# Exponentials issued one block product behind the minima of their scores, in a fused attention and feed-forward kernel

## The chip, the cores and the metric

The kernel runs on one core of one Trainium2 chip. The metric is the time of one execution on the device in microseconds (us), as the median of several runs. The core has five engines that work side by side, each through its own list of instructions: PE (TensorE, matrix products; its weight loads are shown as PEld), DVE (VectorE), ACT (ScalarE), POOL (GpSimd) and SP (SyncE, which here only starts transfers). They wait for each other by semaphores.

## The reference

Sliding-window attention over 8 batches, 8 heads, 576 positions and 64 columns per head is followed by a feed-forward part in which three products are joined by their maximum.

```python
scores = (1/sqrt(64)) * q @ k.T                        # [8, 8, 576, 576]
rel = pos[:, None] - pos[None, :]
scores = where((rel >= 0) & (rel < 128), scores - slope[h] * abs(rel), -1e9)
attn = exp(scores - max(scores)); attn = attn / (sum(attn) + 1e-9)
x = (attn @ v)  -> rows of [4608, 512]
h = maximum(maximum(x @ w1, x @ w2), x @ w3)           # [4608, 768]
out = h @ w_out                                        # [4608, 512]
```

## The kernel before

**Attention.** A batch has four pairs of heads, and each pair five blocks of query rows: four of 128 and one of 64. One such block is a *step*; a batch has 20. For one step the work goes through these functions:

- `products` (L283): PE makes the scores of two blocks at a time, in PSUM. Because the window is 128 wide, each row needs 128 keys, taken from its own block and the one before.
- `score`: DVE merges the two blocks of keys into 128 columns (L298 or L301, a predicated copy), then for each of the two heads adds the bias and takes the row's minimum of the negated scores in one instruction (L313), which writes the tile `s` and one column of `st`. ACT then takes the exponential of `s` into the tile `p`, with that minimum as its bias, and sums each row into `st` (L317). The tiles `s` are a ring of three, the tiles `p` a ring of four.
- `sums_of`: for two blocks (one, for the last of a pair) DVE adds 1e-9 to the sums (L326) and takes reciprocals (L329).
- `normalise`: ACT multiplies `p` by the reciprocals, head by head (L341). In the first two batches POOL does it for half of the blocks (L336).
- `turn`: PE transposes `p` (L350) into the one tile `pt`, ACT copies it out (L354, L360, L363), and POOL cuts the two triangles of the window out of it (L364, L368).
- `mix`: PE multiplies with `v` (L390) into `ps_x`, and ACT copies the finished pair of heads to `xk` (L399).

**Feed-forward.** Each of the matrices is cut in blocks of two by two, and a product is made in seven block products by a scheme of Strassen's kind, so that per batch there are 11 x 7 = 77 *units*. A unit is one block product on PE: six matmuls of 128x288 for w1, w2 and w3, nine for w_out (L541). Numbers are split in a high and a low part: ACT casts the high part (L416), and DVE or POOL subtracts to get the low part (L417). The sums and differences of blocks are DVE's (L420). The results go into three PSUM banks in turn. The first three units of a product are copied out of their bank by ACT (L550), to be added again by DVE later (L490, L504, L507); L499 and L505 take the maximum over w1, w2 and w3, and L488 and L501 are copies on ACT. Unit results for w_out go to memory by SP.

**Weights.** At the start the weights are converted from 64-bit words on ACT and DVE (L137 to L145), split (L151, L152), combined on PE (L162) and stored by SP in device memory as `keep`; the w_out part stays on the core. Each batch after the first loads them again from `keep`, in two pieces per matrix, into a ring of two (L239, issued from POOL's queue when a piece has become free).

**What sets the order.** The program makes a list of events, each with a time in steps, sorts it and issues the work in that order. Step `s` is the block's number plus a shift per batch. `products` come at `s` (for two blocks), `score` at `s + 0.04`, `sums_of` at `s + 0.9`, `normalise` at `s + 1.3`, `turn` four steps behind the products and `mix` some six. The units of the batch before are spread over the same time line, one every 0.285 to 0.32 of a step. A scheduler then orders each engine's instructions, by priorities that follow the order of issue and by when it expects their inputs. From the end of the second batch's attention on PE's order is kept as the program has it (`fix`); the other engines' order stays the scheduler's.

The lines touched are L304 to L320 in `score` and the list of events, L578 to L581; what reads their results is L326, L329, L341 and the transposes L350. The lines that stand beside them on ACT and DVE, and on which PE waits, are L550, L416, L420, L499 and L504.

## Time and profile before

| | us |
|---|---|
| median of 3 runs | 832.92 (832.41 to 834.43) |
| the profiled execution's own time | 837.5 |
| its span in the profile | 835.4 |
| mean granted clock of PE in it | 0.987 of full speed |

The profile is one execution. Its times are in us from the start of the span. A row of the timeline has start, length, engine, line of the kernel, operation, output and input tiles, shapes and the number of instructions (x1), and in brackets how long the engine stood idle before it and which instruction, by engine, tile and line, released it. A row of the waits has the engine with the line that waited, what it waited for, and then us in total, number of waits and the longest. Rows of a table by stretches have the stretch, its length, and busy time with the number of instructions for each engine. A busy PE need not run at its peak, since the ends of its matmuls are modelled.

One batch takes 92.4 us in the steady part. The stages in the span: weights are prepared up to about 205 us, beside the attention of the first batches; the first batch's units for w1 to w3 run to about 280; four like batches follow from 320 to 690; from 690 the last one runs out. A matmul of L541 has a mean of 299 ns, an exponential L317 of 401 ns, a copy L550 of 395 ns.

### The profile page before, as it was taken

What the parts mean: (1) busy time and instruction counts of PE and PEld (TensorE: products, weight loads), DVE (VectorE), ACT (ScalarE), POOL (GpSimd) and SP (SyncE); (2) the same over time, 40 slices, a digit from 0 to 9 for tenths busy, and PEclk for the clock granted to TensorE, in tenths of its full rate; (3) what the DMA queues carried; (4) which work ended last, traced back from release to release, by engine and by line L of the source; (5) the groups of instructions that cost most, each with busy time, mean ns of one, the idle gap of its engine ahead of it and who ended that gap; (6) DMA issues with size and microseconds to landing.
All of it is one profiled execution on the core that took longest, in us unless ns stands there. A gap on an engine that the chain in (4) does not pass through costs nothing.

```text
span 835.4 us, 18318 instructions
## 1 busy us (share of the span) xinstructions
PE 786.7 (94%) x6488; PEld 692.4 (83%) x6488; DVE 564.2 (68%) x1758; ACT 530.3 (63%) x1728; POOL 325.1 (39%) x564
## 2 busy tenths in 40 slices
PE   4987999999999999999999999999999999999988
PEld 2555888789888898889888988889888899899987
DVE  5768999985666846775667847694767747674452
ACT  6779887865667756676557756775657666552332
POOL 2333252532345515542345416541444425531332
PEclk9969999999999999999999999999999999999999
DMA  7664378475877548783687558873787458656751
GB/s 250 212 229 133 125 284 291 164 265 163 266 267 265 192 151 282 261 274 126 232 290 256 195 196 273 273 263 127 245 280 253 170 190 269 246 186 201 272 172 57
DMA packets 43402, 184.81 MB, mean 221 GB/s; under 512 B 4784, under 2 KB 13744, under 8 KB 34096
## 3 DMA queue, kind: packets, MB, share of 16 engines
q0 software_dynamic: 18144, 115.61, 41.7%
q1 hardware_dynamic: 25024, 67.97, 23.1%
q8 instruction: 51, 0.84, 0.4%
q14 instruction: 39, 0.32, 0.1%
q10 hardware_dynamic: 144, 0.07, 0.0%
HBM read 157.68 MB, written 25.95 MB: 220 GB/s over the span
## 4 chain that ended last, share of the span: by engine, by line
PE 63%; DVE 12%; ACT 8%; DMA 6%; issue 5%; POOL 5%; SPq 0%; ACTq 0%; DVEq 0%; POOLq 0%
PE ps_m L541 43%; PE ps_x L390 7%; PE ps_s L283 5%; DMA wt<-keep 4%; PE pt L350 4%; POOL hs L417 4%; PE pt L162 3%; ACT p L317 2%; DVE t L420 2%; DMA hs<-in_w_all 2%; DVE t L504 2%; DVE hq L505 1%; PE ps_m L283 1%; DVE hq L420 1%; ACT p L341 1%
## 5 line engine op out<-in xcount | busy, mean ns | idle before, releaser
L541 PE MATMUL ps_m<-xs,wt 128*128 128x288 f32 x3024 | 435.1, 299 | 16.7 <-ACT t L550 5.4
L541 PEld LDWEIGHTS ps_m<-xs,wt 128*128 128x128 f32 x3024 | 409.1, 189 | 27.7 <-ACT t L550 7.5
L550 ACT COPY t<-ps_m 128x288 f32<-128x288 f32 x264 | 103.0, 395 | 84.4 <-PE ps_m L541 83.5
L364 POOL TENSOR_SCALAR_AFFINE_SELECT pp<-pr 128x256 f32<-128x256 f32 (+1 forms) x128 | 54.9, 429 | 244.3 <-ACT pr L363 143.3
L541 PE MATMUL ps_m<-hs,ow 128*128 128x288 f32 x1008 | 141.6, 297 | 7.1 <-POOL hs L417 3.4
L541 PEld LDWEIGHTS ps_m<-hs,ow 128*128 128x128 f32 x1008 | 134.5, 188 | 10.7 <-POOL hs L417 4.5
L317 ACT ACTIVATE p<-s,st 128x128 f32<-128x128 f32 (+1 forms) x320 | 127.2, 401 | 17.7 <-DVE st L313 12.1
L239 POOL DMA_DIRECT2D wt<-keep x126 | 70.1, 556 | 133.9 <-PE ps_m L541 124.1
L417 POOL TENSOR_TENSOR hs<-hq,hs 128x288 fp32r<-128x288 f32 x88 | 78.1, 896 | 67.7 <-ACT hs L416 67.3
L341 ACT ACTIVATE p<-p,st 128x128 f32<-128x128 f32 x280 | 96.8, 396 | 11.8 <-DVE st L329 11.8
L504 DVE TENSOR_TENSOR t<-ps_m,t 128x288 f32<-128x288 f32 x144 | 64.6, 453 | 49.3 <-PE ps_m L541 34.8
L313 DVE CUSTOM_DVE_ANT_0 s<-ps_s,bias 128x128 f32<-128x128 f32 (+1 forms) x300 | 76.7, 281 | 18.6 <-PE ps_s L283 12.5
L301 DVE COPY_PREDICATED ps_s<-prev,ps_s 128x256 f32<-128x256 uint8 x120 | 50.8, 423 | 50.2 <-PE ps_s L283 48.7
L390 PE MATMUL ps_x<-pp,v 128*64 128x256 f32 (+3 forms) x768 | 82.4, 332 | 1.8 <-POOL pp L364 1.4
L283 PE MATMUL ps_s<-qk 64*64 64x192 f32 (+1 forms) x1080 | 71.4, 333 | 6.3 <-DMA qk<-in_qk 4.2
L390 PEld LDWEIGHTS ps_x<-pp,v 128*64 128x64 f32 (+1 forms) x768 | 46.5, 140 | 28.1 <-issue 12.5
L505 DVE TENSOR_TENSOR hq<-t,hq 128x288 f32<-128x288 f32 x144 | 67.7, 478 | 2.4
L363 ACT COPY pr<-pt 128x256 f32<-128x256 f32 x64 | 18.9, 321 | 74.6 <-PE pt L350 74.6
L417 POOL TENSOR_TENSOR hs<-t,hs 128x288 fp32r<-128x288 f32 x64 | 58.9, 924 | 15.2 <-ACT hs L416 14.9
L350 PE MATMUL pt<-ident,p 128*128 128x128 f32 (+1 forms) x320 | 56.6, 289 | 7.6 <-POOL p L336 3.9
L317 ACT ACTIVATION_READ_ACCUMULATOR p<-s,st 128x1 f32 (+1 forms) x320 | 61.7, 193 | 0.0
L283 PEld LDWEIGHTS ps_s<-qk 64*64 64x64 f32 x1080 | 41.4, 136 | 23.6 <-issue 10.9
(68 smaller groups left out, 837.8 us busy)
## 6 DMA issues: line engine op xcount, KB each, us to landing
wt<-keep POOLq DMA_DIRECT2D x63, 1024.0 KB, 7.7
wt<-keep POOLq DMA_DIRECT2D x63, 768.0 KB, 5.0
qk<-in_qk SPq DMA_DIRECT2D x31, 576.0 KB, 5.4
hs<-in_w_all SPq DMA_DIRECT2D x24, 512.0 KB, 3.9
v<-in_v SPq DMA_DIRECT2D x32, 320.0 KB, 4.2
keep<-wt SPq DMA_DIRECT2D x9, 1024.0 KB, 5.1
outT<-t SPq DMA_DIRECT2D x64, 144.0 KB, 1.8
keep<-wt SPq DMA_DIRECT2D x9, 768.0 KB, 3.6
```

Source lines behind the costliest of these rows:

```text
L239: nc.gpsimd.dma_start(wts[n, a], keep[n % 9][a])
L283: pe(nc.tensor.matmul(ps[j][d:d + D, o:o + k1 - k0], lhsT=qkt[t][j * D:(j + 1) * D, 0, q0:q0 + D], rhs=qkt[t][j * D:(j + 1) * D, 1, k0:k1] ...
L313: nc.vector.tensor_tensor_reduce(out=s[:n], in0=ps[j][:n, P:2 * P], in1=(bias if i else bias0)[:n, 2 * hp + j, :], scale=-0.125, scalar=3. ...
L317: nc.scalar.activation(p[:n, j], s[:n], AF.Exp, bias=st[:n, 0, a, j:j + 1], scale=-1.0, accum_out=st[:n, 1, a, j:j + 1])
L341: nc.scalar.activation(p[:n, j], p[:n, j], AF.Copy, scale=st[:n, 2, a, j:j + 1])
L350: pe(nc.tensor.transpose(out=pt[:, a, j, :n], in_=p[:n, j], identity=ident[:n, :n]))
L390: pe(nc.tensor.matmul(x[j * D:(j + 1) * D, c:c + e - a], lhsT=vv[:n, i, j * D:(j + 1) * D], rhs=w[:n, j].rearrange("p a b -> p (a b)")[:, ...
L417: e.tensor_tensor(out=lo, in0=src, in1=hi.bitcast(F32), op=ALU.subtract)
L504: nc.vector.tensor_tensor(out=s, in0=ps, in1=e, op=ALU.add)
L505: nc.vector.tensor_tensor(out=h, in0=s, in1=h, op=ALU.max)
L541: pe(nc.tensor.matmul(ps, lhsT=lt, rhs=rt, start=i == 0 and k in (0, 1, 4), stop=i == len(pairs) - 1, skip_group_check=True,))
L550: nc.scalar.copy(out=e, in_=ps)
```

## The change

`score` keeps the merging and the two minima, and puts the two tiles `s` aside. A new function `exps` takes the tile `p` and issues the two exponentials. It is an event of its own at `s + 0.3`, where before the exponentials came at `s + 0.04` with the minima. With units about 0.3 of a step apart this lets one unit be issued between a block's minima and its exponentials. `sums_of` moves from `s + 0.9` to `s + 1.1` and `normalise` from `s + 1.3` to `s + 1.5`. Operations, sizes and rings stay the same.

```diff
-        p = s_p.tile([P, 2, P], F32, name="p", bufs=4)
...
         a = len(two)
-        two.append(p)
+        two.append(None)
+        less[t, i] = []
         for j in range(2):
             s = s_p.tile([P, P], F32, name="s", bufs=3)
             nc.vector.tensor_tensor_reduce(
...
             )
+            less[t, i].append(s)
+
+    less = {}
+
+    def exps(t, i):
+        n = rows[i]
+        st, two = stats[t, i // 2]
+        a = i % 2
+        p = two[a] = pn[t, i] = s_p.tile([P, 2, P], F32, name="p", bufs=4)
+        for j, s in enumerate(less.pop((t, i))):
             nc.scalar.activation(
                 p[:n, j], s[:n], AF.Exp, bias=st[:n, 0, a, j:j + 1], scale=-1.0, accum_out=st[:n, 1, a, j:j + 1]
             )
-        pn[t, i] = p
...
             at(s + 0.04, score, t, i)
+
+            at(s + 0.3, exps, t, i)
             if i % 2 or i + 1 == NB:
-                at(s + 0.9, sums_of, t, i)
-                at(s + 1.3, normalise, t, i)
+                at(s + 1.1, sums_of, t, i)
+                at(s + 1.5, normalise, t, i)
```

The added lines shift later ones by nine or ten: L317 becomes L327, L326 and L329 become L335 and L338, L341 becomes L350, L350 becomes L359, L399 becomes L408, L416 becomes L425, L420 becomes L429, L499 becomes L508, L504 and L505 become L513 and L514, and L550 becomes L559. In the steady batches PE's and SP's order is the same before and after, but for a load of `qk` and one of weights at three places on SP, in the preparing stage. ACT's and DVE's order differs at five places of each batch, of which three follow. Rows have the line, the operation, output and input tiles, the size, and x2 for two in a row; numbers at a tile's name tell tiles of one name apart.

First, ACT in a steady batch, where the 64-row block of a pair of heads is scored while the units of a product run (around 513 us in the profile). Before:

```order
L363 COPY pr<-pt 128x256
L317 ACTIVATE p,st<-s,st 64x128 x2
L550 COPY t<-ps_m_5787 128x288
L317 ACTIVATE p,st<-s,st 128x128 x2
L341 ACTIVATE p<-p,st 64x128 x2
L550 COPY t<-ps_m_5913 128x288
```

After:

```order
L372 COPY pr<-pt 128x256
L327 ACTIVATE p,st<-s,st 64x128
L559 COPY t<-ps_m_5787 128x288
L327 ACTIVATE p,st<-s,st 64x128
L327 ACTIVATE p,st<-s,st 128x128 x2
L350 ACTIVATE p<-p,st 64x128 x2
L559 COPY t<-ps_m_5910 128x288
```

The copy out of the bank `ps_m_5787` has moved ahead of the block's second exponential.

Second, ACT where the units of w_out begin and the next batch's factors `xs` are cast (around 557 us). Before:

```order
L363 COPY pr<-pt 128x256
L416 CAST xs<-xk_4874 128x576
L317 ACTIVATE p,st<-s,st 64x128 x2
L416 CAST hs_5156<-t_5098 128x288
L550 COPY t<-ps_m_5164 128x288
L550 COPY t<-ps_m_5180 128x288
L416 CAST hs_5212<-hq 128x288
L317 ACTIVATE p,st<-s,st 128x128 x2
```

After:

```order
L372 COPY pr<-pt 128x256
L425 CAST xs<-xk_4872 128x576
L425 CAST hs_5151<-t_5098 128x288
L559 COPY t<-ps_m_5159 128x288
L327 ACTIVATE p,st<-s,st 64x128 x2
L559 COPY t<-ps_m_5176 128x288
L425 CAST hs_5210<-hq 128x288
L327 ACTIVATE p,st<-s,st 128x128 x2
```

A cast and the first of the two copies have moved ahead of both exponentials; the second copy stays behind them.

Third, DVE where a 64-row block's minima, the sums of two blocks and the maximum of two products meet (around 530 to 535 us). Before:

```order
L326 TENSOR_SCALAR st<-st 128x4
L504 TENSOR_TENSOR t<-ps_m_4664,t 128x288
L505 TENSOR_TENSOR hq<-t,hq 128x288 x2
L420 TENSOR_TENSOR t_4764<-hq 128x288
L329 RECIPROCAL st<-st 128x4
L313 ISA s,st<-ps_s,bias 64x128
L313 ISA st 64x1
L420 TENSOR_TENSOR t_4765<-hq,t_4764 128x288
L420 TENSOR_TENSOR hq<-hq 128x288
L313 ISA s,st<-ps_s,bias 64x128
L313 ISA st 64x1
L499 TENSOR_TENSOR hq<-ps_m_4664,hq 128x288
```

After:

```order
L313 ISA s,st<-ps_s,bias 64x128
L313 ISA st 64x1
L514 TENSOR_TENSOR hq<-t,hq 128x288
L513 TENSOR_TENSOR t<-ps_m_4662,t 128x288
L429 TENSOR_TENSOR t_4761<-hq 128x288
L514 TENSOR_TENSOR hq<-t,hq 128x288
L313 ISA s,st<-ps_s,bias 64x128
L313 ISA st 64x1
L429 TENSOR_TENSOR t_4762<-hq,t_4761 128x288
L429 TENSOR_TENSOR hq<-hq 128x288
L335 TENSOR_SCALAR st<-st 128x4
L508 TENSOR_TENSOR hq<-ps_m_4662,hq 128x288
```

Both minima have moved up, the addition to the sums (L326, now L335) has moved from the front to just ahead of the maximum L508, and the reciprocal (L329, now L338) behind it.

## The prediction

> **What bounds the kernel now.** I read the page first, then the engines' busy time by stretches, then what TensorE (PE) waits for, and last its timeline through one batch.

> ```profile
> PE 786.7 (94%) x6488; PEld 692.4 (83%) x6488; DVE 564.2 (68%) x1758; ACT 530.3 (63%) x1728; POOL 325.1 (39%) x564
> PEclk9969999999999999999999999999999999999999
> wt<-keep POOLq DMA_DIRECT2D x63, 1024.0 KB, 7.7
> ...
> 0.00:80.00 80.00, 60.12 (x404) 37.30 (x404) 56.07 (x210) 60.94 (x196) 26.79 (x53) 0.89 0.59 205
> 80.00:160.00 80.00, 75.53 (x595) 62.93 (x594) 75.52 (x208) 66.03 (x190) 32.70 (x46) 1.00 0.62 223
> 320.00:690.00 370.00, 361.73 (x3141) 326.06 (x3141) 248.13 (x811) 240.76 (x824) 155.16 (x277) 1.00 0.69 233
> ```

> The columns behind the length are busy PE, weight loads, DVE, ACT, POOL, then PE's clock and the DMA share. From 320 to 690 us, four batches long, PE is busy 361.73 of 370 us: only 8.3 us can go there without fewer matmuls, and the change removes none. Before 160 us, while the weights are prepared, PE is idle 19.9 and 4.5 us of 80, and from 80 to 160 us DVE is as busy as PE (75.52). So the change can act through PE's short stalls in the steady batches, and through other engines in the preparing stage.

> ```profile
> PE ps_m L541 <- ACT t L550: 4.2, 8, 0.6
> PE ps_m L541 <- DVE hq L499: 1.6, 4, 0.4
> PE ps_m L541 <- DVE t L504: 1.4, 2, 0.8
> PE ps_m L541 <- DMA wt<-keep: 1.0, 2, 0.7
> ...
> 513.65 4.26 PE L541 MATMUL ps_m<-xs,wt 128*128 128x288 f32 x30 [0.59 <-ACT t L550]
> 522.09 4.22 PE L541 MATMUL ps_m<-xs,wt 128*128 128x288 f32 x30 [0.38 <-DMA wt<-keep]
> 534.75 1.06 PE L541 MATMUL ps_m<-xs,wt 128*128 128x288 f32 x6 [0.39 <-DVE hq L499]
> 558.70 5.15 PE L541 MATMUL ps_m<-hs,ow 128*128 128x288 f32 x36 [0.46 <-ACT t L550]
> 565.00 8.51 PE L541 MATMUL ps_m<-hs,ow 128*128 128x288 f32 x63
> ```

> The first four rows are PE's waits from 320 to 690 us (total, times, longest): 8.2 of its 8.3 idle us. The others place them in one batch (start, length, in brackets the wait before). The batch repeats every 92.4 us, and each has the same four stalls. I call the places A (513.65), B (522.09), C (534.75), D (558.70), and E the run of 63 at 565.00, without a stall so far. Eight waits on L550 in four batches are two per batch, at A and D: ACT is late with the copy that empties a product's bank.

> **The change part by part.** No engine gets another operation: 320 exponentials, as many sums and normalisations, the same matmuls. PE's order is unchanged behind the preparing stage. What moves is order on ACT and DVE.

> *Place A.* The 64-row block's second exponential stood ahead of the copy:

> ```profile
> 512.84 0.39 ACT L317 ACTIVATE p<-s,st 64x128 f32<-64x128 f32 x1
> 513.23 0.37 ACT L550 COPY t<-ps_m 128x288 f32<-128x288 f32 x1
> ```

> Now the copy goes first, so it ends 0.39 us earlier and the stall of 0.59 falls to 0.20. But what is late next, 8 us on, is the weights transfer at B:

> ```profile
> 512.91 1.50 POOL hs L417 x2
> 514.42 7.54 DMA wt<-keep
> 522.09 1.03 PE ps_m L541 x6
> ...
> 337.51 2.77 PE L541 MATMUL ps_m<-xs,wt 128*128 128x288 f32 x19 [0.60 <-DVE t L504]
> 329.63 0.58 POOL L239 DMA_DIRECT2D wt<-keep  x1
> ```

> The first three rows are the chain of waits up to B: POOL's casts, the transfer issued behind them, 7.54 us long, and PE. POOL's order is unchanged at this place, so the transfer ends when it did, and what PE gains at A it waits at B. In the batch at 337.51 the row names L504, yet its transfer, issued at 329.63 and 7.7 us long by the page, lands at 337.3, just as late. So A is worth **0** in these four batches. The first and the last batch have stalls of A's kind too:

> ```profile
> 230.37 3.46 PE L541 MATMUL ps_m<-xs,wt 128*128 128x288 f32 x24 [0.61 <-ACT t L550]
> 254.41 3.46 PE L541 MATMUL ps_m<-xs,wt 128*128 128x288 f32 x24 [0.72 <-ACT t L550]
> 280.31 3.61 PE L541 MATMUL ps_m<-hs,ow 128*128 128x288 f32 x24 [0.58 <-ACT t L550]
> 285.06 1.84 PE L541 MATMUL ps_m<-hs,ow 128*128 128x288 f32 x12 [1.14 <-POOL hs L417]
> 698.38 1.86 PE L541 MATMUL ps_m<-xs,wt 128*128 128x288 f32 x12 [0.57 <-ACT t L550]
> ```

> No late transfer follows at 230, 254 and 698: one exponential each, 3 x 0.39 = **1.2 us**. What is won at 280.31 is lost again at 285.06, where POOL is late by itself: 0.

> *Place D.* Both 64-row exponentials stood ahead of the pair of copies:

> ```profile
> 557.14 0.41 ACT L317 ACTIVATE p<-s,st 64x128 f32<-64x128 f32 x1
> 557.54 0.40 ACT L317 ACTIVATE p<-s,st 64x128 f32<-64x128 f32 x1
> 557.92 0.42 ACT L416 CAST hs<-t 128x288 fp32r<-128x288 f32 x1
> 558.25 0.69 ACT L550 COPY t<-ps_m 128x288 f32<-128x288 f32 x2
> ```

> Now cast and first copy go ahead of both, 558.25 - 557.14 - 0.33 (the cast's step) = 0.78 us earlier. That is more than the stall of 0.46, which goes whole: 4 x 0.46 = **1.85 us**. Next on ACT are the two exponentials and the second copy, due one product of nine matmuls later (1.2 us), with 0.8 us ahead of it: covered.

> *Place C.* PE waits for L499 on DVE. The reciprocal L329 leaves its place ahead of it, and the first minimum is issued earlier; but L326 comes in just before it:

> ```profile
> 531.51 0.45 DVE L420 TENSOR_TENSOR t<-hq 128x288 f32<-128x288 f32 x1
> 531.88 0.17 DVE L329 RECIPROCAL st<-st 128x4 f32<-128x4 f32 x1
> 532.01 1.79 POOL L417 TENSOR_TENSOR hs<-hq,hs 128x288 fp32r<-128x288 f32 x2 [2.28 <-ACT hs L416]
> 533.06 1.06 DVE L420 TENSOR_TENSOR hq<-hq 128x288 f32<-128x288 f32 x1
> ```

> Bounds per batch: 0 (L326, of L329's size at its shortest, takes what L329 gave back) to the stall, 0.39. I take 0.2, the nearer to the 0.17 that the reciprocal leaves free: 4 x 0.2 = **0.8 us**. The subtraction L420 takes 0.45 us by itself and 1.06 beside POOL's casts, so the order of these two engines can eat it. [...]

> *Place E.* Here the change costs something. In the run of 63 a copy moves one exponential back:

> ```profile
> 567.48 0.38 ACT L550 COPY t<-ps_m 128x288 f32<-128x288 f32 x1
> ```

> It ends at 567.86. The run's fourth product needs it, at 565.00 + 27 x 8.51/63 = 568.65: a margin of 0.79. The exponential takes 0.39 and PE, 0.46 earlier through D, takes the rest: -0.06, so I put 4 x 0.1 = **-0.4 us**.

> *Sums and normalisation.* They come 0.2 of a step later; a step is 92.4/20 = 4.62 us, so 0.92 us. Transposes that read the result stand at fixed places of PE's order, at least half a step (2.3 us) behind: 0. On POOL one weights transfer is issued behind two more casts at C, some 0.6 us later. Of PE's waits on transfers there are two in four batches, 1.0 us, the one shown at B (0.38) and its like, so none falls to this transfer: 0. Without that cover it would cost up to 0.6 us a batch, 2.4 in all.

> *The preparing stage.* Order changes at many places, on PE too, so no row prices it.

> ```profile
> 14.35 0.69 ACT L141 ACTIVATE hs<-hs 128x512 int32<-128x512 f32 x1
> ...
> DVE s L313 <- ACT p L317: 3.7, 6, 1.4
> ...
> 49.60:53.00 3.40, 3.40 (x27) 2.15 (x24) 1.07 (x3) 2.77 (x10) 1.75 (x4) 0.50 0.51 152
> ```

> The first row is a weights conversion that now can stand ahead of an exponential; the second, DVE's waits up to 205 us, shows that the minima already wait for the exponentials to free one of three s tiles; the third shows half clock with PE busy throughout. The page's third slice (41.8 to 62.7 us) has 0.6, which is what 13 to 17 of its 20.9 us at half clock would give; at most half of that is lost by it. Bounds: -8 (that stretch gone) to +7 (the rival below). Reasons exist for both signs; I take **0**.

> **Sum**: -1.2 - 1.85 - 0.8 + 0.4 = -3.4 us. The profiled execution took 837.5 us (span 835.4 and 2.1 around it), so 834.1; it was 4.6 us above the median of the runs, 832.92, and the forecast for the median is **829.5**.

> **Rivals.**

> *No change.* D's gain may be taken like A's: PE reaches the next late transfer or DVE result earlier and waits there. For it: at B this happens by the rows above, and the DMA share is 0.69. Against it: behind D no stall stands before the next batch's A. What is left is the 1.2 us of first and last batch less E's 0.4: 832.1.

> *Slower, through the preparing stage.* There the exponentials wait on ACT behind a conversion of 0.69 us, the s ring of three holds up the next minima, and DVE has no room. Between 80 and 160 us DVE handles 15 blocks:

> ```profile
> 80.00:160.00 80.00, 7.75 (x60) 1.00 0.62 223
> ```

> (60 L313 rows, four per block.) If every block pays, 15 x 0.69 = +10.4 - 3.4 = +7.0: 839.9. It undoes the gain from 5 blocks on and makes the kernel measurably slower from 9. For it: DVE is busy 75.52 of 80 us and already waited 3.7 us for L317. Against it: ACT was busy only 66.03, and a conversion's room exists. At 11 blocks it gives +4.2: 837.1.

> *Faster by more.* If the reordering fills PE between 41.8 and 62.7 us so that the half clock ends 8 us earlier, up to 4 us come on top: 825.5. For it: PE is busy in that stretch, and half clock doubles its time. Against it: what starts the slow stretch is the missing work before it. [...]

> **How the numbers follow.** A measurement of this kernel tells about 0.3%, 2.5 us, from no change: the bounds are 830.4 and 835.4. Forecast 0.50 (its own range 827.5 to 831.5, of which 0.32 below 830.4 and 0.18 above); no change 0.20; slower 0.15; faster by more 0.15. Faster 0.32 + 0.15 = 0.47; same 0.18 + 0.20 + 0.02 of the slower case where few blocks pay = 0.40; slower 0.13. The range 825.5 to 835.5 takes in the half of "faster by more" that stays small, "no change", and C's and E's bounds; it leaves out most of "slower" and the rest of "faster by more", 0.2.

> **What would show it.** At D no wait for ACT's copy, and 558.70's run 0.46 us closer to its forerunner. At A a wait of some 0.2 us and at B one longer by 0.39. At C a wait for L508 (the old L499) between 0 and 0.39. At E a wait of 0.1 or none. A batch that repeats every 91.9 us or so, where 92.4 stood. Up to 205 us the same time within 1 us, with DVE's waits for the exponentials near 3.7 us. The forecast is wrong if the period of the batches stays, or if the steady part starts more than 2.5 us earlier or later.

## The result and the profile after

The changed kernel took 855.0 us (median of 3 runs, 853.93 to 856.78) against 832.92 before: a ratio of 1.0245, with a 95% interval of 1.0206 to 1.0283. It is slower by 2.5%, where the prediction was 829.5 us, slightly faster. The profiled execution after the change took 855.0 us, its span 852.9.

First the busy time by stretches of the changed kernel (columns as before: PE, weight loads, DVE, ACT, POOL, PE's clock, DMA share, GB/s), then what PE waits for from 320 to 690 us.

```profile
0.00:80.00 80.00, 57.45 (x400) 36.06 (x401) 56.49 (x211) 61.96 (x198) 25.03 (x53) 0.88 0.60 205
80.00:160.00 80.00, 75.61 (x577) 62.87 (x577) 70.85 (x199) 63.48 (x180) 32.51 (x44) 0.95 0.62 218
320.00:690.00 370.00, 354.30 (x3015) 318.02 (x3014) 248.65 (x785) 236.74 (x804) 154.96 (x270) 0.99 0.66 224
...
PE ps_m L550 <- DVE hq L508: 9.2, 4, 2.3
PE ps_m L550 <- POOL hs L426: 3.2, 8, 0.5
PE ps_m L550 <- DVE hq L514: 1.2, 1, 1.2
PE ps_m L550 <- DMA wt<-keep: 1.2, 2, 0.8
PE ps_m L550 <- ACT t L559: 0.8, 4, 0.2
```

PE's idle time in the steady part grew from 8.3 to 15.7 us. The waits for ACT's copy fell from 4.2 us in eight to 0.8 in four, as forecast: D's are gone and A's are 0.2 each. But the four waits for L508 (before: L499), 1.6 us in all, are now 9.2. All of them are at C. The timeline at C follows, as start, length and instruction, in three parts: DVE, PE, and POOL.

```profile
540.91 1.06 DVE L429 TENSOR_TENSOR hq<-hq 128x288 f32<-128x288 f32 x1
541.89 2.63 DVE L335 TENSOR_SCALAR st<-st 128x4 f32<-128x4 f32 x1
544.44 0.45 DVE L508 TENSOR_TENSOR hq<-ps_m,hq 128x288 f32<-128x288 f32 x1
...
544.94 1.06 PE L550 MATMUL ps_m<-xs,wt 128*128 128x288 f32 x6 [2.31 <-DVE hq L508]
545.93 1.93 PE L399 MATMUL ps_x<-pp,v 128*64 128x256 f32 x14
...
541.60 0.58 POOL L239 DMA_DIRECT2D wt<-keep  x1
542.20 0.81 POOL L426 TENSOR_TENSOR hs<-t,hs 128x288 fp32r<-128x288 f32 x1
542.96 1.53 POOL L426 TENSOR_TENSOR hs<-hq,hs 128x288 fp32r<-128x288 f32 x2
```

The addition of 1e-9 to 128x4 sums, L335, lasts 2.63 us. It begins while POOL issues a transfer, and it ends (544.52) 0.03 us after the last of three subtractions that POOL runs without a gap (544.49). In the other four batches it is the same, to 0.01 us. Elsewhere the same instruction takes 0.15 to 0.17 us when POOL does nothing. In the kernel before, the same addition stood some 4 us ahead of the maximum and was short, and the 14 matmuls behind the maximum (L390 there) were faster:

```profile
529.98 0.16 DVE L326 TENSOR_SCALAR st<-st 128x4 f32<-128x4 f32 x1
...
535.74 1.19 PE L390 MATMUL ps_x<-pp,v 128*64 128x256 f32 x14
```

The change put the addition just ahead of L508, for which PE waits. Then a second loss begins. The 14 matmuls, now of L399, take 1.93 us behind the wait in place of 1.19. The granted clock shows why, here for the stretches right behind it:

```profile
545.00:547.00 2.00, 2.00 (x14) 1.50 (x16) 1.36 (x5) 2.00 (x7) 1.31 (x2) 0.78 0.19 71
547.00:549.00 2.00, 2.00 (x29) 1.34 (x25) 0.00 (x0) 1.38 (x4) 0.79 (x1) 0.50 0.76 188
549.00:550.00 1.00, 1.00 (x9) 1.00 (x8) 0.85 (x5) 0.32 (x2) 0.00 (x0) 0.74 1.10 442
```

PE is busy throughout, at half clock for some 3.4 us. In the kernel before, the clock was full from 320 to 690 us.

Since PE's order is the same behind the preparing stage, the matmuls of both traces can be paired, and the difference of their starts grows only where time is lost. From some 340 us on to the last batch's end of its units for w1 to w3 it goes from 2.3 to 19.2 us:

| place | a batch, us | in all, us |
|---|---|---|
| C, the wait itself | 1.9, five times | +9.6 |
| C, half clock behind it | 1.5 to 1.6, in four of five | +6.1 |
| D | -0.6, four times | -2.5 |
| E | +1.1, four times | +4.4 |
| the rest, A and B | | -0.7 |

The preparing stage can't be paired so. There a matmul group that both programs have at the same place of PE's order serves as a mark: the eight of L390 (after: L399) that start at 224.64 us before the change and at 227.87 after it.

### The profile page after: what moved, and what is told of

It reads as the page before. It is cut to its first block, busy times and chain, and to the rows that moved or that the text cites. A ratio compares the mean times of both kernels' runs of the same rounds, so it can differ in the third digit from the quotient of the medians.

```text
span 852.9 us, 18326 instructions
## 1 busy us (share of the span) xinstructions
PE 795.2 (93%) x6488; PEld 698.5 (82%) x6488; DVE 570.8 (67%) x1758; ACT 534.2 (63%) x1728; POOL 328.0 (38%) x564
## 4 chain that ended last, share of the span: by engine, by line
PE 61%; DVE 17%; ACT 7%; POOL 5%; issue 5%; DMA 4%; SPq 0%; ACTq 0%; DVEq 0%; POOLq 0%
PE ps_m L550 41%; PE ps_x L399 7%; PE ps_s L283 5%; POOL hs L426 4%; PE pt L359 4%; DMA wt<-keep 3%; PE pt L162 3%; DVE t L429 2%; DVE t L513 2%; DVE st L335 2%; DVE hq L514 2%; ACT p L327 1%; DVE s L313 1%; DVE ps_s L301 1%; DVE hq L429 1%
## 5 line engine op out<-in xcount | busy, mean ns | idle before, releaser
L550 PE MATMUL ps_m<-xs,wt 128*128 128x288 f32 x3024 | 439.2, 301 | 21.5 <-DVE hq L508 11.5
L550 PEld LDWEIGHTS ps_m<-xs,wt 128*128 128x128 f32 x3024 | 412.1, 190 | 33.9 <-DVE hq L508 12.9
L559 ACT COPY t<-ps_m 128x288 f32<-128x288 f32 x264 | 104.0, 394 | 77.9 <-PE ps_m L550 76.9
L550 PE MATMUL ps_m<-hs,ow 128*128 128x288 f32 x1008 | 143.5, 298 | 8.2 <-POOL hs L426 6.1
L550 PEld LDWEIGHTS ps_m<-hs,ow 128*128 128x128 f32 x1008 | 134.9, 188 | 12.6 <-POOL hs L426 9.1
L327 ACT ACTIVATE p<-s,st 128x128 f32<-128x128 f32 (+1 forms) x320 | 127.4, 401 | 17.2 <-DVE st L313 11.8
L239 POOL DMA_DIRECT2D wt<-keep x126 | 69.8, 554 | 131.5 <-PE ps_m L550 124.3
L426 POOL TENSOR_TENSOR hs<-hq,hs 128x288 fp32r<-128x288 f32 x88 | 81.0, 927 | 68.8 <-ACT hs L425 68.5
L350 ACT ACTIVATE p<-p,st 128x128 f32<-128x128 f32 x280 | 95.3, 396 | 11.4 <-DVE st L338 10.8
L513 DVE TENSOR_TENSOR t<-ps_m,t 128x288 f32<-128x288 f32 x144 | 64.7, 452 | 48.2 <-PE ps_m L550 39.0
L313 DVE CUSTOM_DVE_ANT_0 s<-ps_s,bias 128x128 f32<-128x128 f32 (+1 forms) x300 | 76.7, 284 | 25.1 <-PE ps_s L283 19.9
L399 PE MATMUL ps_x<-pp,v 128*64 128x256 f32 (+3 forms) x768 | 84.6, 344 | 2.4 <-POOL pp L373 2.1
L399 PEld LDWEIGHTS ps_x<-pp,v 128*64 128x64 f32 (+1 forms) x768 | 48.3, 146 | 29.6 <-issue 12.1
L514 DVE TENSOR_TENSOR hq<-t,hq 128x288 f32<-128x288 f32 x144 | 69.6, 487 | 2.5
L359 PE MATMUL pt<-ident,p 128*128 128x128 f32 (+1 forms) x320 | 57.0, 288 | 11.8 <-POOL p L345 4.7
L426 POOL TENSOR_TENSOR hs<-t,hs 128x288 fp32r<-128x288 f32 x64 | 59.3, 930 | 14.4 <-ACT hs L425 14.1
L359 PEld LDWEIGHTS pt<-ident,p 128*128 128x128 f32 (+1 forms) x320 | 34.3, 143 | 36.3 <-issue 20.5
L425 ACT CAST hs<-hq 128x288 fp32r<-128x288 f32 x96 | 40.6, 431 | 35.3 <-DVE hq L514 17.6
## 6 DMA issues: line engine op xcount, KB each, us to landing
wt<-keep POOLq DMA_DIRECT2D x63, 1024.0 KB, 7.3
keep<-wt SPq DMA_DIRECT2D x9, 1024.0 KB, 5.7
```

Source lines behind the costliest of these rows:

```text
L239: nc.gpsimd.dma_start(wts[n, a], keep[n % 9][a])
L313: nc.vector.tensor_tensor_reduce(out=s[:n], in0=ps[j][:n, P:2 * P], in1=(bias if i else bias0)[:n, 2 * hp + j, :], scale=-0.125, scalar=3. ...
L327: nc.scalar.activation(p[:n, j], s[:n], AF.Exp, bias=st[:n, 0, a, j:j + 1], scale=-1.0, accum_out=st[:n, 1, a, j:j + 1])
L350: nc.scalar.activation(p[:n, j], p[:n, j], AF.Copy, scale=st[:n, 2, a, j:j + 1])
L359: pe(nc.tensor.transpose(out=pt[:, a, j, :n], in_=p[:n, j], identity=ident[:n, :n]))
L399: pe(nc.tensor.matmul(x[j * D:(j + 1) * D, c:c + e - a], lhsT=vv[:n, i, j * D:(j + 1) * D], rhs=w[:n, j].rearrange("p a b -> p (a b)")[:, ...
```

## The experiments

Two theories stood at the start. Theory 1: the moved *sums* are what costs, by that one addition at C. Theory 2: the late *exponentials* cost, by what stands behind them on ACT. A rival to both was the preparing stage. "Before" is the kernel before the change, run again beside each group: 835.04 us (19 runs), 834.64 (25) and 836.54 (13). Its runs spread from 829.65 to 839.22 us, so single medians count only to a few us. A ratio weighs all runs of both kernels, with its 95% interval in brackets; where a difference in us is given beside it, it is the ratio's, which can lie up to 2 us off the difference of the medians.

**Exponentials late, sums at their old time.**

```diff
-                at(s + 1.1, sums_of, t, i)
-                at(s + 1.5, normalise, t, i)
+                at(s + 0.9, sums_of, t, i)
+                at(s + 1.3, normalise, t, i)
```

> Exponentials late (s + 0.3), sums and normalisation at their old times. Theory 1 (the moved addition L335 is what costs: at C it stands just ahead of the maximum L508 and lasts 2.63 us beside POOL's casts, then PE runs some us at half clock): with the sums back, the addition leaves that place, so C's wait is at most 0.4 us and no half clock follows; 9.6 + 5.8 us of the changed kernel's loss go, 836 to 841 us is left. Theory 2 (the exponentials being late is what costs): 850 to 856, as the changed kernel.

Measured: 838.49 us, 1.0046 of before (1.0016 to 1.0077). Theory 1's range holds it. Most of the loss went with the sums. E takes part in what is left, some 4 us: with the matmuls paired as above it costs 1.1 us a batch here too, and PE's waits from 320 to 690 us hold 3.3 us for POOL in eight, though the sums are early.

**Sums and normalisation late, exponentials at their old place.** The kernel before with `s + 1.1` and `s + 1.5`.

> Exponentials early as before, sums and normalisation late (s + 1.1 and s + 1.5). Theory 1: the addition stands just ahead of the maximum at C as in the changed kernel, lasts some 2.6 us there, PE waits 2.3 us and runs at half clock behind it: 845 to 852 us. Theory 2: no more than 836, as before.

Measured: 853.57 us, 1.0246 (1.0193 to 1.0299), a little above theory 1's range: the whole loss of the change without its main part. Its waits from 320 to 690 us:

```profile
PE ps_m L541 <- DVE hq L499: 9.2, 4, 2.3
PE ps_m L541 <- ACT t L550: 4.2, 8, 0.6
```

C has the long wait, and the waits for ACT at A and D are what they were. No wait for POOL at E is on the list. Theory 2 falls as the main cause: the late exponentials take away the second row and bring the waits at E, the late sums make the first row.

**A reciprocal in place of the addition.** This tells the place from the kind of operation.

```diff
-        nc.vector.tensor_scalar(
-            out=st[:n, 1, :a + 1], in0=st[:n, 1, :a + 1], scalar1=1e-9, scalar2=None, op0=ALU.add
-        )
+        nc.vector.reciprocal(st[:n, 2, :a + 1], st[:n, 1, :a + 1])
         nc.vector.reciprocal(st[:n, 2, :a + 1], st[:n, 1, :a + 1])
```

> The changed kernel with the addition of 1e-9 (L335) taken out and a second reciprocal of the same size put in its place, so that DVE has as many instructions at the same places. The sums are then taken without the 1e-9. Theory 1, if it is the kind of operation that waits for POOL: reciprocals last 0.15 to 0.17 us there, C's wait falls under 0.4 us, the half clock goes, 834 to 840 us. Rival: any DVE instruction at that place waits for POOL's casts: 2 us or more at C, 850 to 856.

Measured: 831.14 us, 0.9966 (0.9935 to 0.9997), 3 us under theory 1's range and far from the rival's. The place C in this run, DVE and then POOL:

```profile
528.68 0.16 DVE L335 RECIPROCAL st<-st 128x4 f32<-128x4 f32 x1
528.77 0.42 DVE L506 TENSOR_TENSOR hq<-ps_m,hq 128x288 f32<-128x288 f32 x1
...
528.39 0.58 POOL L239 DMA_DIRECT2D wt<-keep  x1
528.98 0.83 POOL L424 TENSOR_TENSOR hs<-t,hs 128x288 fp32r<-128x288 f32 x1
529.76 2.30 POOL L424 TENSOR_TENSOR hs<-hq,hs 128x288 fp32r<-128x288 f32 x3
```

The reciprocal of the same 128x4 numbers stands ahead of the maximum in the same way, POOL issues its transfer and is about to run its subtractions as before, and it lasts 0.16 us. So it is the kind of operation, not the place in the order, that made DVE wait for POOL here: the addition took 2.63 us, over a transfer's issue and three of POOL's subtractions in a row, and the reciprocal in its place 0.16. The traces of the kernel before and of the changed one agree: in neither does a reciprocal take more than 0.18 us, and 18 and 9 of the 96 in each run beside a subtraction of POOL's (L417, now L426), at no more than 0.17.

**The change from the third batch on.** Preparing stage as before, steady batches as in the changed kernel (`exps`, `sums_of` and `normalise` at their new times only for `b > 1`).

> The change from the third batch on only, so that the preparing stage (PE's order wholly as before) is unchanged. By the traces the preparing stage costs 3.1 us of the loss: 849 to 852 us by theory 1. If the preparing stage is the main cause (rival): 836 to 842.

Measured: 849.54 us, 1.0183 (1.0141 to 1.0224), or 15 us. The steady batches are the main cause.

**The change in the first two batches only,** the reverse of the last (`b < 2`).

> The reverse of the run that changes from the third batch on: the change in the first two batches only, so the preparing stage as in the changed kernel and the steady batches as before. If the loss of the preparing stage is real, 3 to 7 us above the kernel before of the same call, 836 to 842. If it was a chance of the profiled execution (rival): within 1.5 us of the kernel before.

Measured: 838.35 us, 1.0061 (1.0035 to 1.0087), or 5 us; 15 and 5 make nearly the 21 of the whole. The preparing stage's loss is real. The mark on PE's timeline stands as follows in the kernel before, the changed one, the change from the third batch on, and the change in the first two only:

```profile
224.64 1.08 PE L390 MATMUL ps_x<-pp,v 128*64 128x256 f32 x8
...
227.87 1.08 PE L399 MATMUL ps_x<-pp,v 128*64 128x256 f32 x8
...
221.23 1.08 PE L399 MATMUL ps_x<-pp,v 128*64 128x256 f32 x8
...
227.36 1.08 PE L399 MATMUL ps_x<-pp,v 128*64 128x256 f32 x8
```

First and third have PE's work in the same order up to there and differ by 3.4 us, so this stage varies by that much from run to run. Over more traces the two kinds still lie apart: the mark is at 221.2, 224.6 and 225.5 us in the three with the first two batches as before (the third is the run with one sum late), and at 226.7 to 230.7 in the five with the whole change in them. The profile of before comes from an execution of 837.5 us, longer than the median; that is why the two profiles lie only 17.5 us apart and the medians 21 to 22.

**The changed kernel once more,** unedited.

> The changed kernel once more, unedited, beside the others on one chip, for a second profile: 852 to 857 us. If the half clock behind C follows from the wait there, it is seen in four or five of five batches again, each 1.3 to 1.5 us; if it was chance, at other places.

Measured: 855.62 us, 1.0256 (1.0222 to 1.0291). The wait at C is there five times, and half clock behind it again in four of five, though not in the same four. It was missing behind the second in the first profile and behind the fourth in this one; the last section shows why.

**The changed kernel without the addition.** The reciprocals read the sums without the 1e-9.

> The changed kernel without the addition of 1e-9 (L335); the reciprocals read the sums of the exponentials as they are. Theory 1 (the addition's wait for POOL is the loss in the steady batches, at C and at E): no wait over 0.4 us at C, no half clock behind it, 828 to 834 us, as with two reciprocals (831.1). Rival (what helped there was that something still stood ahead of L508): 836 or more.

Measured: 832.29 us, 0.9963 (0.9935 to 0.9992). It falls in theory 1's range, and no wait for the maximum at C is left in the list of waits:

```profile
PE ps_m L547 <- DMA wt<-keep: 2.5, 3, 1.1
PE ps_m L547 <- ACT t L556: 2.1, 4, 0.6
PE ps_m L547 <- POOL hs L423: 1.2, 4, 0.3
```

The third row also speaks of E. The changed kernel waited eight times there, 3.2 us; without the addition it is four waits and 1.2 us.

**The kernel before without the addition.**

> The kernel before without the addition of 1e-9. There the addition's longest are 1.28 us, behind L499 and so off PE's path. Theory 1: little to win, 0 to 4 us below the kernel before of the same call. If additions cost time all over the kernel (rival): 5 us or more.

Measured: 831.18 us, 0.9946 (0.9919 to 0.9974), 4.5 us below before: at the edge between theory and rival, so the additions cost something before the change too. Part of it shows in the trace from 320 to 690 us: PE's waits for the maximum at C (1.6 us) and for L504 (1.4 us) are gone, and those for ACT have grown from 4.2 to 5.4 us. Where the rest went stays open.

**One sum per batch late.** This puts C alone to the test.

```diff
-                at(s + 0.9, sums_of, t, i)
+                at(s + (1.1 if b > 1 and hp == 3 and i == 3 else 0.9), sums_of, t, i)
```

> The kernel before with one sum per batch moved, that of blocks 2 and 3 of the last pair of heads, from the third batch on, from s + 0.9 to s + 1.1; everything else early as before. Five times it then stands just ahead of the maximum at C. Theory 1: 2.6 us long there, five waits of 2.3 us in place of 0.4 and half clock behind four or five of them, 9.6 + 5.8 us: 13 to 17 us above the kernel before of the same call. Rival (the loss comes from the change as a whole, no single place): under 5 us above.

Measured: 847.19 us, 1.0141 (1.0078 to 1.0204), 6.5 to 17 us with 11.8 in the middle: somewhat less than I expected, well above the rival. By the middle value, one moved addition per batch is over half of the whole loss. The four waits for the maximum from 320 to 690 us are the changed kernel's, to the digit:

```profile
PE ps_m L541 <- DVE hq L499: 9.2, 4, 2.3
```

**The same sum early, all else late.** The changed kernel with `0.9 if b > 1 and hp == 3 and i == 3 else 1.1`.

> The changed kernel with only that one sum per batch back at s + 0.9. Theory 1: 13 to 17 us below the changed kernel (855.0 and 855.6), 838 to 843 us; what is left above the kernel before is E (1.1 us a batch) and the preparing stage. Rival: 850 or more.

Measured: 843.34 us, 1.0101 (1.0048 to 1.0154), 12 us below the changed kernel, at the edge of theory 1's range; 5 us of the rest are the preparing stage's, and E's waits for POOL remain (3.3 us in eight).

**PE kept at work through the wait.** The changed kernel with matmuls that nobody reads ahead of the product that waits at C.

```diff
+        if u % 77 == 47 and 2 <= b <= 6:
+            fill = ps_t.tile([P, 2, 2, P], F32, name="pt").rearrange("p a b c -> p (a b c)")[:, :C]
+            for _ in range(15):
+                pe(nc.tensor.matmul(fill, lhsT=ow[:, 0, 0, 0, :P], rhs=pairs[0][1], start=True, stop=True, skip_group_check=True))
```

> The changed kernel with 15 matmuls of 128x288 (some 2.0 us) that nobody reads, issued on PE ahead of the product that waits at C, five times in all, so that PE works while it would wait. Theory: the half clock behind C follows from PE's idle time there; the wait for L508 shrinks to some 0.3 us, PE is as late as before, and the half clock goes, 5 to 7 us below the changed kernel, 848 to 851 us. Rival (the clock falls for another reason, such as the bursts of work around): half clock stays, 853 to 858 us.

Measured: 849.22 us, 1.017 (1.0121 to 1.0219), 6 us below the changed kernel. PE's timeline at C, the addition beside it, and the clock behind:

```profile
539.73 2.14 PE L549 MATMUL pt<-xs,ow 128*128 128x288 f32 x15
542.25 1.06 PE L554 MATMUL ps_m<-xs,wt 128*128 128x288 f32 x6 [0.38 <-DVE hq L508]
...
539.16 2.68 DVE L335 TENSOR_SCALAR st<-st 128x4 f32<-128x4 f32 x1
...
543.00:545.00 2.00, 2.00 (x36) 1.35 (x34) 1.23 (x3) 2.00 (x8) 1.22 (x3) 1.00 0.50 120
```

The addition is as long as ever and PE no earlier with the product, but the clock stays at 1.00 at all five places. So the half clock of the changed kernel follows from PE's idle time in the wait of 2.3 us; with 0.38 us idle it did not come.

**Late exponentials, old sums, no addition.** The best combination that the other runs suggested.

> Exponentials late, sums at their old time and without the addition of 1e-9. The gain at D (0.5 us a batch) stays and the addition can't stand in the way anywhere: 828 to 832 us, 0.3 to 0.8% below the kernel before of the same call, like the kernel before without the addition or 1 to 2 us better. If it isn't better than that one, the late exponentials by themselves are worth nothing.

Measured: 831.68 us, 0.9943 (0.991 to 0.9977). It is faster than both kernels, and so is the kernel before without the addition (0.9946). The two can't be told apart, so without the additions the late exponentials are worth nothing that can be measured; with them they cost 0.2 to 0.8% (the first run). Every sum is at least 1, because the largest score gives exp(0) = 1, and in 32 bits 1 + 1e-9 rounds to 1, so by this arithmetic leaving the addition out changes no number.

## Why the prediction was wrong

- **C is the step that failed.** I bounded it at 0 on the bad side with the words "L326, of L329's size at its shortest, takes what L329 gave back". That priced the addition by a neighbour of another kind. The trace of before had a row of this very operation at this very place, in its 64-row form:

```profile
534.89 1.29 DVE L326 TENSOR_SCALAR st<-st 64x2 f32<-64x2 f32 x1 [0.19 <-ACT p L317]
```

  It was harmless there, behind L499. It, too, ended 0.03 us after a subtraction of POOL's that ran beside it (536.14). Since the order showed L326 moving to just ahead of L499, this row had to price the move. With three of POOL's subtractions in a row it became 2.63. The prediction did see DVE held beside POOL (L420, 1.06 us for 0.45), but let that eat no more than the gain. Measured: a loss of 9.6 us where I had a gain of 0.8.
- **A second loss was missed.** I looked for half clock only in the preparing stage. A wait of 2.3 us brings it in the steady part as well: 6.1 us.
- **A**: the wait fell from 0.59 to 0.20 as worked out, but B did not take the gain back as I had it. In each of the four batches from 320 us on, 0.23 of the 0.39 us was lost again in the run of 30 matmuls right behind A (4.25 us before, 4.48 after). PE's waits at B, for weights and for L504, changed by -0.4 to +0.6 us from batch to batch and are 2.4 us in all before and after (with L514 in L504's place). Together A and B gained some 0.9 us in these batches where I had 0.
- **The first batch** gained 0.9 us between 221 and 255 us, forecast 0.8. **D** gained 0.6 a batch, forecast 0.46. Both mechanisms were right.
- **E** was mis-sized: 1.1 us a batch where I had 0.1, and not by the copy that I named. PE came 0.6 us earlier through D and met POOL's subtractions (L426), which had not moved. Then the 64-row addition, now behind L508, held DVE for 0.49 us, and the subtraction of POOL's at 572.56 took 1.62 us where it had taken 1.14:

```profile
571.08 2.66 PE L550 MATMUL ps_m<-hs,ow 128*128 128x288 f32 x18 [0.30 <-POOL hs L426]
574.23 1.85 PE L550 MATMUL ps_m<-hs,ow 128*128 128x288 f32 x12 [0.49 <-POOL hs L426]
...
571.94 0.49 DVE L335 TENSOR_SCALAR st<-st 64x2 f32<-64x2 f32 x1
572.34 0.74 DVE L426 TENSOR_TENSOR xs<-xk,xs 128x576 fp32r<-128x576 f32 x1
```

  The runs with late exponentials and no addition bear out the second part: they keep only the first wait of each batch (1.2 us for POOL in place of 3.2). The first is "no change" in small: D's gain taken by what is late next. Both come with the late exponentials, not with the late sums, since the first run has them and the second has none.
- **The preparing stage** was put at 0 with +7 as the bad end; it cost 5. The mechanism of the rival "slower", minima that wait for the exponentials through the ring of three, is not it: DVE waited for L327 there no longer than before (up to 230 us, 3.7 us before, 2.3 after). What grew is the wait of the sums for the late exponentials, before the change and after it:

```profile
DVE st L326 <- ACT p L317: 2.1, 4, 1.0
...
DVE st L335 <- ACT p L327: 5.1, 9, 1.0
```

  That these 3 us make the 5 is not borne out. With a reciprocal in place of the addition the same wait is 5.7 us, and yet the mark on PE's timeline stands at 223.2, among those of the unchanged stage; with the addition left out it stands at 224.9. So this loss, too, seems to hang on the addition, though none lasts more than 0.78 us up to 205 us. By which waits it costs there stays open.
- **The chances**: slower had 0.13, for a mechanism that did not appear. The range had no room for a loss at C, whose bounds ran from 0 to a gain of 0.39 a batch: its upper end, 835.5, lies 19.5 us under the 855.0 measured.

## What to carry to other kernels

Moving a tiny instruction in an engine's order can cost more than the large one it was moved for: here an addition of 0.16 us took 2.63 at its new place, and the waits there cost 9.6 us, where the late exponentials gained 2.5 at D. Price it by the longest rows of the same operation in the trace, not by its size or by its mean, and look at what another engine does beside those longest rows. When a move puts something just ahead of the instruction that the critical engine waits for, its worst row is the price. And a wait of some 2 us on PE can cost more than half of its length again in the clock behind it: here 1.5 us for 2.3.
